# Decay attention with a gated convolution: loads in separate buffers, x's low part in two pieces, another order of the steps

## The chip, the core and the metric

The kernel runs on one core of a Trainium2 chip. A core has a tensor engine for matrix products (PE in the profile, its weight loads PEld), three engines for elementwise work (DVE, ACT and POOL), and a sync engine (SP), which here only issues the transfers between HBM and the core's SBUF. Matrix products land in PSUM, which has eight banks. The engines run side by side and wait for each other by semaphores. The metric is the device time in microseconds (us) of one execution.

## What is computed

Decayed linear attention over blocks of 64 positions, for 4 batches, 8 heads, 768 positions and head dimension 64; then, over the 512 channels that the heads make together, a causal convolution of 5 taps whose sigmoid gates `x @ w_val`, and a last product with `w_out`. `w_val`, `conv_w` and `w_out` come as float64, q, k, v and lam as float32.

```python
for b in range(nb):                                   # blocks of 64 positions
    intra = einsum('bhic,bhjc->bhij', qb, kb) * Dmask # lam^(i-j), lower triangle
    intra = einsum('bhij,bhjd->bhid', intra, vb)
    inter = einsum('bhid,bhde->bhie', qb * lam_pow, kv_state)
    out[:, :, sl] = intra + inter
    kv_state = lam_block * kv_state + einsum('bhsd,bhse->bhde', kb * rev_pow, vb)
...
x = out.transpose(0, 2, 1, 3).reshape(B, S, 512)
gate = sigmoid(sum(conv_w[k] * xp[:, k:k + S] for k in range(5)))
return (gate * (x @ w_val)) @ w_out
```

## The kernel before

The work is cut into 12 chunks (i = 0 to 11): chunk i holds 128 positions of one pair of batches, chunks 0 to 5 of the first pair and 6 to 11 of the second, where the state starts anew. Two chunks make a unit (un = 0 to 5), over which the convolution runs.

Every step is an entry of a plan with a name, an engine and the steps that it needs. The names, which the text below uses:

- `ld.i.0` and `ld.i.2` load 1 MB each: q and k transposed (kT), and v and k by positions. `wv.u` and `wo.u` load the halves of the weights, 1 MB each, and `cv` conv_w (20 KB).
- `s.i.u` are the scores on PE (`u` is a half of the heads; in chunks 0 to 2 each half is a step), `m.i...` their masking on DVE, `kd.i` the decay of k (on ACT in chunks 1, 2, 3, 4 and 6, otherwise on POOL), `st.i` the product of k and v on PE that updates the state, `up.i` the update on DVE, `fd.i` the fading of the state on POOL, `qd.i` the decayed q on POOL, `ia.i` and `in.i` the products within the block and with the state, on PE, into the bank `xp`.
- `x.i` copies x out of `xp` and `xh.i` makes its high part, both on ACT; `xl.i` is the rest, x minus the high part, on DVE in chunks 0 and 1 and on POOL in the others. The low part makes up for the precision that the fast product of the high part loses: `v.i.f` (256 columns) and `V.un.f` (512 columns) on PE multiply x by w_val as high times high, low times high and high times low, 12 matrix products for a step.
- `wv.u.k.e`, `n`, `s`, `w`, `v` on DVE, `r`, `m`, `h` on ACT and `l` on POOL turn a quarter of the float64 weights into a high part (`h`) and a low part (`l`).
- `t.un.f.kk` are the taps, the first on ACT and four on DVE, `sg` the sigmoid on ACT, `pb` the copy of a product out of PSUM on ACT, `ap` the gating on DVE, `hh` and `hl` the high and low part of the gated value, `p.i...` the product with w_out on PE, `ev` its copy on ACT and `o` its store.
- `f.n` is a filling product of zeros on PE. `WARM` products of zeros stand ahead of everything, and `f.0` and `f.1` between the first scores.

ORDER is a table of all these names, in which the steps are written out one after another. Each engine gets its own steps in that order and does them in that order: a step that waits holds up what is behind it on its engine, and a load on SP that waits for its buffer holds up all later loads and stores. After a colon stand the buffers that a step takes (`ld0`, `s0`, `u2`); it waits until the last reader of what was in them is done. SLOTS says how many there are of each. PSUM has four banks `u`, one `s` and one `xp` in use by name (`xp` and `s` take two banks each).

In the buffer `ld` lie all four parts of a chunk, so that neither of its loads can start before every reader of the chunk that was there is done, the last being the products `st` and `ia`.

## Time and profile before

| | |
|---|---|
| runs | 207.83, 209.11 and 210.05 us, median 209.11 |
| profiled execution | 208.13 us |
| its span, first to last instruction | 206.4 us (1.7 us lie around it) |
| busy: PE, PEld, DVE, ACT, POOL | 97%, 83%, 75%, 56%, 56% of the span |
| TensorE clock granted | 1.00 over the whole span |
| transfers | 36.15 MB; the DMA engines are full from about 5 to 40 us |

The page's first part gives the busy time of each engine. A matrix product's end is modelled, and products overlap; the starts of consecutive rows tell better what one of them takes. The answers are read by their times from the start of the span.

### The profile page before, as it was taken

What the parts mean: (1) busy time and instruction counts of PE and PEld (TensorE: products, weight loads), DVE (VectorE), ACT (ScalarE), POOL (GpSimd) and SP (SyncE); (2) the same over time, 40 slices, a digit from 0 to 9 for tenths busy, and PEclk for the clock granted to TensorE, in tenths of its full rate; (3) what the DMA queues carried; (4) which work ended last, traced back from release to release, by engine and by line L of the source; (5) the groups of instructions that cost most, each with busy time, mean ns of one, the idle gap of its engine ahead of it and who ended that gap; (6) DMA issues with size and microseconds to landing.
All of it is one profiled execution on the core that took longest, in us unless ns stands there. A gap on an engine that the chain in (4) does not pass through costs nothing.

```text
span 206.4 us, 7456 instructions
## 1 busy us (share of the span) xinstructions
PE 199.5 (97%) x3316; PEld 172.2 (83%) x3316; DVE 154.5 (75%) x240; ACT 115.2 (56%) x218; POOL 115.3 (56%) x103
## 2 busy tenths in 40 slices
PE   7879899999999999999999999999999999999995
PEld 7479699998999998989887978887987888888883
DVE  5797997999686999999989667817789289686000
ACT  2277779869664976676634925523565352642121
POOL 5276492788788499949975999662573400000000
DMA  5999999802878005994601159610020002210042
GB/s 174 418 426 422 422 427 426 351 10 67 346 268 345 8 3 157 347 404 124 251 4 54 56 173 391 256 51 3 3 77 27 0 3 102 103 51 0 3 176 79
DMA packets 7952, 36.15 MB, mean 175 GB/s; under 512 B 1136, under 2 KB 1392, under 8 KB 4336
## 3 DMA queue, kind: packets, MB, share of 16 engines
q1 hardware_dynamic: 7920, 35.68, 44.7%
q8 instruction: 26, 0.43, 0.8%
q14 instruction: 6, 0.05, 0.1%
HBM read 29.38 MB, written 6.29 MB: 173 GB/s over the span
## 4 chain that ended last, share of the span: by engine, by line
PE 87%; DMA 8%; SPq 2%; DVE 1%; POOL 1%; issue 0%; ACT 0%
PE op L837 33%; PE vp L728 33%; DMA w_raw<-in_w_val 8%; PE xp L510 5%; PE s L470 4%; PE xp L547 4%; PE st L572 4%; SPq L337 1%; PE xp L525 1%; POOL wv_lo L302 1%; PE so L460 1%; PE xp L536 1%; PE st L564 0%; PE fill L205 0%; DVE w_em L260 0%
## 5 line engine op out<-in xcount | busy, mean ns | idle before, releaser
L702 DVE SCALAR_TENSOR_TENSOR acc<-x,conv_sb,acc 128x512 f32<-128x512 f32 x96 | 70.7, 753 | 8.7 <-ACT acc L700 6.8
L728 PE MATMUL vp<-x_hi,wv_hi 128*128 128x256 f32 (+1 forms) x144 | 47.3, 328 | 0.0
L728 PE MATMUL vp<-x_hi,wv_lo 128*128 128x256 f32 (+1 forms) x144 | 45.9, 319 | 0.5 <-POOL wv_lo L302 0.5
L728 PE MATMUL vp<-x_lo,wv_hi 128*128 128x256 f32 (+1 forms) x144 | 45.8, 318 | 0.0
L844 ACT COPY o<-op 128x512 f32<-128x512 f32 (+1 forms) x25 | 14.3, 571 | 31.3 <-PE op L837 28.8
L676 POOL TENSOR_TENSOR x_lo<-x,x_hi 128x1024 fp32r<-128x1024 f32 x10 | 24.0, 2400 | 12.6 <-ACT x_hi L666 9.1
L837 PE MATMUL op<-wo_hi,hs 128*128 128x512 f32 x96 | 30.6, 400 | 0.0
L728 PEld LDWEIGHTS vp<-x_hi,wv_hi 128*128 128x128 f32 x144 | 27.3, 190 | 3.1 <-issue 0.2
L728 PEld LDWEIGHTS vp<-x_hi,wv_lo 128*128 128x128 f32 x144 | 27.3, 190 | 2.6 <-POOL wv_lo L302 0.7
L728 PEld LDWEIGHTS vp<-x_lo,wv_hi 128*128 128x128 f32 x144 | 27.4, 190 | 1.9
L420 POOL TENSOR_TENSOR qd<-ld,qdec_c 128x512 f32<-128x512 f32 (+1 forms) x18 | 23.4, 1308 | 4.8 <-DMA ld<-in_qkv 4.8
L707 ACT ACTIVATE g<-acc 128x512 f32<-128x512 f32 x24 | 14.4, 600 | 15.0 <-DVE acc L702 15.0
L584 POOL TENSOR_TENSOR sdec<-state,qdec_c 128x512 f32<-128x512 f32 x17 | 18.6, 1096 | 7.1 <-DVE state L581 7.1
L837 PEld LDWEIGHTS op<-wo_hi,hs 128*128 128x128 f32 x96 | 17.4, 188 | 3.9
L810 POOL TENSOR_TENSOR hs<-g,hs 128x512 fp32r<-128x512 f32 x12 | 15.4, 1296 | 9.0 <-ACT hs L799 9.0
L837 PE MATMUL op<-wo_hi,h_hi 128*128 128x512 f32 (+1 forms) x52 | 19.7, 379 | 0.0
L837 PE MATMUL op<-wo_hi,h_lo 128*128 128x512 f32 (+1 forms) x52 | 19.6, 377 | 0.0
L837 PE MATMUL op<-wo_lo,h_hi 128*128 128x512 f32 (+1 forms) x52 | 19.6, 376 | 0.0
L837 PE MATMUL op<-wo_lo,hs 128*128 128x512 f32 x48 | 18.8, 392 | 0.0
L700 ACT ACTIVATE acc<-x,conv_sb 128x512 f32<-128x512 f32 x24 | 16.7, 696 | 3.6 <-DVE state L581 3.2
L581 DVE TENSOR_TENSOR state<-st,sdec 128x512 f32<-128x512 f32 x17 | 11.7, 686 | 6.9 <-PE st L572 3.5
L799 ACT CAST h_hi<-vp 128x512 fp32r<-128x512 f32 x12 | 6.9, 590 | 16.2 <-DVE vp L774 16.2
(77 smaller groups left out, 354.9 us busy)
## 6 DMA issues: line engine op xcount, KB each, us to landing
ld<-in_qkv SPq DMA_DIRECT2D x24, 1024.0 KB, 8.9
out<-o SPq DMA_DIRECT2D x23, 256.0 KB, 2.1
w_raw<-in_w_val SPq DMA_DIRECT2D x2, 1024.0 KB, 11.4
w_raw<-in_w_out SPq DMA_DIRECT2D x2, 1024.0 KB, 14.3
out<-o SPq DMA_DIRECT2D x2, 128.0 KB, 1.7
conv_raw<-in_conv_w SPq DMA_DIRECT2D x1, 20.0 KB, 10.5
lam_bc<-in_lam SPq DMA_DIRECT2D x1, 4.0 KB, 1.7
```

The lines of the kernel that those rows point to most:

```text
L420: nc.gpsimd.tensor_tensor(out=s["qd"][:, hs, ms], in0=lds[i]["qT"][:, u].rearrange("p h (m i) -> p h m i", m=2)[:, :, ms], in1=qdec[:, hs, ...
L510: nc.tensor.matmul(s["xp"][rows(hh), b ^ m, b, g, :], lds[i]["v"][rows(m), b, h * D : (h + 1) * D], s["A"][rows(m), b, h, :], start=b == 0 ...
L581: nc.vector.tensor_tensor(out=state, in0=s["st"][m], in1=sdec, op=ALU.add)
L584: nc.gpsimd.tensor_tensor(out=sdec, in0=state, in1=qdec_c[:, :, n - 1 : n].to_broadcast([P, H, D]), op=ALU.mult)
L676: nc.gpsimd.tensor_tensor(out=s["x_lo"], in0=s["x"], in1=s["x_hi"].bitcast(F32), op=ALU.subtract)
L700: nc.scalar.mul(to, src, w)
L702: nc.vector.scalar_tensor_tensor(out=to, in0=src, scalar=w, in1=to, op0=ALU.mult, op1=ALU.add)
L707: nc.scalar.activation(xu[un]["g"][:, ct].rearrange("p u (b i) -> p b u i", b=NB2), xu[un]["acc", ct].rearrange("p b (u i) -> p b u i", u= ...
L728: nc.tensor.matmul(to, w[:, ct, fs], xx[:, ct], start=n_mm == 0, stop=n_mm == 3 * NT - 1)
L810: (nc.vector if direct else nc.gpsimd).tensor_tensor(out=to, in0=x["h", j, fs], in1=x["to", j, fs].bitcast(F32), op=ALU.subtract)
L837: nc.tensor.matmul(s["op", b, j][:, cols], hh, w[:, ft, cols], start=ft == 0 and n == 0, stop=ft == NT - 1 and n == 2,)
L844: nc.scalar.copy(s["o", b, j][:, cols], s["op", b, j][:, cols])
```

## The change

- The buffer `ld` (three, for all four parts of a chunk) becomes `lq` (q with kT) and `lv` (v with k), three of each; a load waits for the readers of its own half alone.
- `xl.i` on POOL, one subtraction of 1024 columns, becomes `xl.i.0` and `xl.i.1`, of 512 columns each. Every product with w_val still waits for both pieces of its chunk.
- The buffers of the output `o` are three and no longer two. `ident` is made in the buffer of `sdec`, which has no other use at that time.
- One filling product stays of three (FILL); in the new order it stands after both score steps of chunk 0.
- ORDER is another table of the same steps. Both loads of chunk 0 stand ahead of the first half of w_val, and `ld.2.0` ahead of `ld.1.2`.

The diff, cut: of the table one line of each stands here.

```diff
-FILL = 3
+FILL = 1
...
-SLOTS = {"ld": 3, "qd": 2, "A": 2, "x": 3, "xs": 2, "g": 2, "val": 4, "hs": 2, "o": 2, "s": 1, "xp": 1, "u": 4}
+SLOTS = {"lq": 3, "lv": 3, "qd": 2, "A": 2, "x": 3, "xs": 2, "g": 2, "val": 4, "hs": 2, "o": 3, "s": 1, "xp": 1, "u": 4}
...
-ld.0.0:ld0 wv.0:g0 ld.0.2 qe dm.0 ld.1.0:ld1 cv ld.1.2 dm.1 wv.1:g1 ld.2.0:ld2 f.0:u0 s.0.0:s0 f.1:u0 m.0.1.0:A0
+dm.0 ld.0.0:lq0 s.0.0:s0 s.0.1:u0,u1 qe dm.1 m.0.0.0:A0 ld.0.2:lv0 kd.0.0 wv.0:g0 ld.1.0:lq1 m.0.0.1:A1 m.0.1.0 f.0:u2
...
-    ident = const.tile([P, P], F32, name="ident")
+    sdec = const.tile([P, H, D], F32, name="sdec")
+    ident = sdec.rearrange("p h d -> p (h d)")[:, :P]
...
-        ld_buf[i] = Buf("ld")
-
-        cuts = (0, 2, 4)
-        for lo, hi in zip(cuts, cuts[1:]):
-
-            def go(i=i, lo=lo, hi=hi, src=qkv[pair, c]):
-                if i not in lds:
-                    t = buf("ld", "ld", [P, 4, 2, DM])
+        lds[i] = {}
+        for lo, tag in ((0, "lq"), (2, "lv")):
+            ld_buf[i, lo] = Buf(tag)
+
+            def go(i=i, lo=lo, tag=tag, src=qkv[pair, c]):
+                t = buf(tag, tag, [P, 2, 2, DM])
+                if lo:
+                    lds[i].update(v=t[:, :, 0], k=t[:, :, 1])
+                else:
...
-                nc.sync.dma_start(lds[i]["all"][:, lo:hi], src[:, lo:hi])
...
+                    lds[i].update(qT=hd[:, :, 0], kT=hd[:, :, 1])
+                nc.sync.dma_start(t, src[:, lo : lo + 2])
...
-        def split_x_lo(s=s, now=now, blocks=blocks):
+        def split_x_lo(u, s=s, now=now, blocks=blocks):
...
+                ts = slice(HU * u, HU * (u + 1))
                 nc.gpsimd.tensor_tensor(
-                    out=s["x_lo"], in0=s["x"], in1=s["x_hi"].bitcast(F32), op=ALU.subtract
+                    out=s["x_lo"][:, ts], in0=s["x"][:, ts], in1=s["x_hi"][:, ts].bitcast(F32), op=ALU.subtract
                 )
...
-        t_xs = add(f"xl.{i}", "DVE" if now else "POOL", split_x_lo, [t_xhi], x_bufs)
+        if now:
+            t_xs = [add(f"xl.{i}", "DVE", lambda f=split_x_lo: f(0), [t_xhi], x_bufs)]
+        else:
+            t_xs = [add(f"xl.{i}.{u}", "POOL", lambda u=u, f=split_x_lo: f(u), [t_xhi], x_bufs) for u in range(2)]
```

The order in which the program's instructions stand shows three places at the front. First the queue of SP, before (after the first load of `ld` and the first half of w_val, the pair of `ld` rows is v and k of chunk 0 and then q and kT of chunk 1):

```order
L173 DMA lam_bc<-in_lam 128x8
L337 DMA ld<-in_qkv 128x2048
L355 DMA w_raw<-in_w_val 128x2048
L337 DMA ld<-in_qkv 128x2048 x2
L370 DMA conv_raw<-in_conv_w 128x40
L337 DMA ld<-in_qkv 128x2048
L355 DMA w_raw<-in_w_val 128x2048
```

The same queue in the changed kernel (`lq` is q with kT, `lv` is v with k; the pair is chunks 1 and 2):

```order
L174 DMA lam_bc<-in_lam 128x8
L337 DMA lq<-in_qkv 128x2048
L337 DMA lv<-in_qkv 128x2048
L355 DMA w_raw<-in_w_val 128x2048
L337 DMA lq<-in_qkv 128x2048 x2
L337 DMA lv<-in_qkv 128x2048
L370 DMA conv_raw<-in_conv_w 128x40
L355 DMA w_raw<-in_w_val 128x2048
```

The first half of w_val moved from the second to the third megabyte, the second half from the sixth to the seventh, and the first load of chunk 1 stayed the fourth.

Second, PE's queue from its start, before (`s` and `so` are the scores of the two halves of the heads, `xp` at L525 the product within the block, `st` the update, `vp` the product with w_val):

```order
L186 MATMUL warm<-zero 128x128 x9
L205 MATMUL fill<-zero 128x512
L460 MATMUL s<-ld 128x128 x8
L205 MATMUL fill<-zero 128x512
L460 MATMUL so<-ld 128x128 x8
L525 MATMUL xp<-A,ld 64x128 x16
L564 MATMUL st<-ld 64x64 x16
L460 MATMUL s<-ld 128x128 x8
L460 MATMUL so<-ld 128x128 x8
L728 MATMUL vp<-x_hi,wv_hi 128x256
```

PE's queue in the changed kernel:

```order
L460 MATMUL s<-lq 128x128 x8
L460 MATMUL so<-lq 128x128 x8
L206 MATMUL fill<-zero 128x512
L525 MATMUL xp<-A,lv 64x128 x16
L460 MATMUL s<-lq 128x128 x8
L564 MATMUL st<-lv 64x64 x16
L460 MATMUL so<-lq 128x128 x8
L460 MATMUL s<-lq 128x128 x8
L460 MATMUL so<-lq 128x128 x8
L525 MATMUL xp<-A,lv 64x128 x16
L536 MATMUL xp<-qd,state 64x128 x16
L564 MATMUL st<-lv 64x64 x16
```

The first product with w_val (`vp`) now stands behind the scores of chunk 2 and all of the attention of chunk 1, and the first scores of chunk 1 stand ahead of the update of chunk 0.

Third, DVE's queue behind the masks of the decay, before (`A` is the masked scores, `w_em` and `w_v` belong to the conversion of w_val):

```order
L483 TENSOR_TENSOR A<-s,mask_c 128x512 x2
L260 TENSOR_SCALAR w_em<-w_raw 128x512
L267 TENSOR_SCALAR w_em<-w_raw 128x512
L483 TENSOR_TENSOR A<-so,mask_c 128x512
L280 SCALAR_TENSOR_TENSOR w_em<-w_raw,w_em 128x512
L267 TENSOR_SCALAR w_em<-w_raw 128x512
L483 TENSOR_TENSOR A<-so,mask_c 128x512
L286 SCALAR_TENSOR_TENSOR w_v<-w_raw,w_v 128x512
L292 TENSOR_TENSOR w_em<-w_v,w_em 128x512
```

DVE's queue in the changed kernel, from the row after the last of the four maskings of chunk 0:

```order
L261 TENSOR_SCALAR w_em<-w_raw 128x512
L268 TENSOR_SCALAR w_em<-w_raw 128x512 x2
L261 TENSOR_SCALAR w_em<-w_raw 128x512
L281 SCALAR_TENSOR_TENSOR w_em<-w_raw,w_em 128x512
L287 SCALAR_TENSOR_TENSOR w_v<-w_raw,w_v 128x512 x2
L293 TENSOR_TENSOR w_em<-w_v,w_em 128x512
L281 SCALAR_TENSOR_TENSOR w_em<-w_raw,w_em 128x512
L483 TENSOR_TENSOR A<-s,mask_c 128x512
L293 TENSOR_TENSOR w_em<-w_v,w_em 128x512
L483 TENSOR_TENSOR A<-s,mask_c 128x512
L579 COPY state<-st 128x512
L672 TENSOR_TENSOR x_lo<-xp,x_hi 128x4x128 x2
```

The four maskings of chunk 0 are now done before the first row of w_val, and the two quarters of the first half of w_val are converted one into the other ahead of the first masking of chunk 1.

Behind the front, PE's order has the attention products in fewer and longer stretches: counted over the whole queue, the products with w_val and w_out (L728 and L837) stand in 22 runs before and in 18 after, of which 2 and 1 lie in the front.

## Rows read from the trace of the kernel before

**Rows 1.** The page's first part: busy us (share) xinstructions.

```profile
PE 199.5 (97%) x3316; PEld 172.2 (83%) x3316; DVE 154.5 (75%) x240; ACT 115.2 (56%) x218; POOL 115.3 (56%) x103
```

**Rows 2.** What PE waited for: us in total, times, longest us.

```profile
PE xp L525 <- DMA ld<-in_qkv: 1.7, 1, 1.7
...
PE s L460 <- DMA ld<-in_qkv: 0.7, 2, 0.5
...
PE xp L510 <- issue: 0.4, 1, 0.4
```

**Rows 3.** PE, front: start us, us, what, xcount [idle before <-releaser].

```profile
6.22 1.16 PE L460 MATMUL s<-ld 64*128 64x128 f32 x16 [0.18 <-DMA ld<-in_qkv]
7.32 1.13 PE L205 MATMUL fill<-zero 128*128 128x512 f32 x2
...
11.34 1.97 PE L525 MATMUL xp<-A,ld 128*64 128x128 f32 x32 [1.67 <-DMA ld<-in_qkv]
...
20.99 1.10 PE L536 MATMUL xp<-qd,state 64*64 64x128 f32 x32
...
24.68 0.39 PE L728 MATMUL vp<-x_hi,wv_lo 128*128 128x256 f32 x1 [0.49 <-POOL wv_lo L302]
...
27.16 1.16 PE L470 MATMUL s<-ld 64*64 64x64 f32 x64
```

**Rows 4.** The transfer of the first half of w_val: start; then its us to landing.

```profile
1.64 0.42 SPq L355 DMA_DIRECT2D w_raw<-in_w_val  x1
...
w_raw<-in_w_val SPq DMA_DIRECT2D x1, 1024.0 KB, 7.1
```

**Rows 5.** DVE, front.

```profile
7.43 1.29 DVE L483 TENSOR_TENSOR A<-s,mask_c 128x512 f32<-128x512 f32 x2 [0.88 <-PE s L460]
8.78 0.43 DVE L260 TENSOR_SCALAR w_em<-w_raw 128x512 int32<-128x512 int32 x1
9.12 0.42 DVE L267 TENSOR_SCALAR w_em<-w_raw 128x512 int32<-128x512 int32 x1
...
20.13 0.76 DVE L260 TENSOR_SCALAR w_em<-w_raw 128x512 int32<-128x512 int32 x2 [1.30 <-DMA w_raw<-in_w_val]
```

**Rows 6.** ACT, front and after it.

```profile
11.93 1.23 ACT L236 COPY dmask<-mask_c 64x512 f32<-64x512 f32 x2
13.34 1.07 ACT L664 CAST x_hi<-xp 128x512 fp32r<-128x512 f32 x2 [0.17 <-PE xp L525]
...
16.73 2.46 ACT L401 ACTIVATE ld<-ld,mask_c 128x128 f32<-128x128 f32 x8
...
28.27 0.31 ACT L272 ACTIVATE w_em<-w_em,rebias 128x20 int32<-128x20 int32 x1 [1.45 <-DVE w_em L260]
...
41.63 0.62 ACT L298 CAST wo_hi<-w_em 128x512 fp32r<-128x512 f32 x1 [1.35 <-DVE w_em L292]
```

**Rows 7.** POOL, front.

```profile
13.77 1.28 POOL L413 TENSOR_TENSOR qd<-ld,qdec_c 128x512 f32<-128x512 f32 x1 [0.35 <-DMA ld<-in_qkv]
```

**Rows 8.** Chain that ended last, in order of time: start us, us, what.

```profile
54.01 1.63 PE vp L728 x12
55.64 0.62 PE xp L547 x32
56.27 0.47 PE xp L510 x32
56.73 7.39 PE vp L728 x60
```

**Rows 9.** POOL's groups: xcount, busy us, mean ns.

```profile
L676 POOL TENSOR_TENSOR x_lo<-x,x_hi 128x1024 fp32r<-128x1024 f32 x10 | 24.0, 2400 | 12.6 <-ACT x_hi L666 9.1 <-PE st L572 3.6
...
L810 POOL TENSOR_TENSOR hs<-g,hs 128x512 fp32r<-128x512 f32 x12 | 15.4, 1296 | 9.0 <-ACT hs L799 9.0
```

**Rows 10.** The end of the span: ACT's last row.

```profile
203.35 0.37 ACT L844 COPY o<-op 128x256 f32<-128x256 f32 x1 [0.85 <-PE op L837]
```

**Rows 11.** One microsecond in which PE stands still: busy us (instructions) by engine, clock.

```profile
10.00:11.00 1.00, 0.00 (x0) 0.00 (x0) 1.00 (x3) 0.45 (x1) 0.00 (x0) 1.00 1.03 434
```

More of the change, by code (lines that the diff above doesn't have):

```diff
@@ new lines @@
+hlw.4.0 p.7.1.0.0:u1 p.7.1.0.1 t.5.0.0:u2,g1 t.5.0.1 t.5.0.2 t.5.0.3 t.5.0.4 ev.7.1.0:o1 p.8.0.0.0:u3 t.5.1.0:u0
+o.7.1.0 t.5.1.1 t.5.1.2 t.5.1.3 p.8.0.0.1 o.6.0.0 ev.8.0.0:o2 sg.5.0 p.8.1.0.0:u1 p.8.1.0.1 ev.8.1.0:o1 p.9.1.0.0:u3
+p.9.1.0.1 t.5.1.4 sg.5.1 t.5.2.0:u2 t.5.3.0:u1 xl.10.1 o.8.1.0 ev.9.1.0:o0 o.9.1.0 t.5.3.1 t.5.2.1 t.5.3.2 t.5.3.3
+t.5.3.4 t.5.2.2 t.5.2.3 p.9.0.0.0:u0 t.5.2.4 p.9.0.0.1 sg.5.3 sg.5.2 ev.9.0.0:o1 xl.11.1 xl.10.0 V.5.0:u3 o.9.0.0
+apw.5.0 hhw.5.0:hs1 hlw.5.0:val3 V.5.1:u1 apw.5.1 hhw.5.1 V.5.2:u2 V.5.3:u0 o.8.0.0 hlw.5.1 apw.5.2 hhw.5.2
@@ L87 @@
+p.11.0.0.0:u3 hlw.5.2:val2 apw.5.3 p.10.0.0.0:u1 hhw.5.3 hlw.5.3 p.10.0.0.1 ev.10.0.0:o0 o.10.0.0 p.10.1.0.0:u2
+p.10.1.0.1 ev.10.1.0:o1 p.11.0.0.1 ev.11.0.0:o2 p.11.1.1.0:u0 p.11.1.1.1 o.10.1.0 o.11.0.0 p.11.1.0.0:u1 p.11.1.0.1
+ev.11.1.1:o0 o.11.1.1 ev.11.1.0:o1 o.11.1.0
 """
@@ L324, in plan_load @@
         pair, c = divmod(i, NC)
-        ld_buf[i] = Buf("ld")
-        cuts = (0, 2, 4)
-        for lo, hi in zip(cuts, cuts[1:]):
-            def go(i=i, lo=lo, hi=hi, src=qkv[pair, c]):
-                if i not in lds:
-                    t = buf("ld", "ld", [P, 4, 2, DM])
-                    hd = t.rearrange("p a w (h i) -> p a w h i", h=HP)
-                    lds[i] = {
-                        "all": t, "qT": hd[:, 0:2, 0], "kT": hd[:, 0:2, 1], "v": t[:, 2:4, 0], "k": t[:, 2:4, 1],
-                    }
-                nc.sync.dma_start(lds[i]["all"][:, lo:hi], src[:, lo:hi])
-            t = add(f"ld.{i}.{lo}", "DMA", go, [], [ld_buf[i]])
-            for part in range(lo, hi):
+        lds[i] = {}
[6 more added lines that the diff above has]
+                else:
+                    hd = t.rearrange("p a w (h i) -> p a w h i", h=HP)
+                    lds[i].update(qT=hd[:, :, 0], kT=hd[:, :, 1])
+                nc.sync.dma_start(t, src[:, lo : lo + 2])
+            t = add(f"ld.{i}.{lo}", "DMA", go, [], [ld_buf[i, lo]])
+            for part in range(lo, lo + 2):
                 t_ld[i, part] = t
@@ L435, in decay_attention_then_gated_conv @@
         t_qd = [
-            add(f"qd.{i}.{u}", "POOL", lambda u=u, f=scale_q: f(u), [t_ld[i, u], *t_qdec], [ld_buf[i], qd_buf])
+            add(f"qd.{i}.{u}", "POOL", lambda u=u, f=scale_q: f(u), [t_ld[i, u], *t_qdec], [ld_buf[i, 0], qd_buf])
             for u in range(0 if big and first else 2)
@@ L473, in scores @@
                             )
-            t_s = add(f"s.{i}.{us[0]}", "PE", scores, [t_ld[i, u] for u in us], [ld_buf[i], *s_bufs])
+            t_s = add(f"s.{i}.{us[0]}", "PE", scores, [t_ld[i, u] for u in us], [ld_buf[i, 0], *s_bufs])
             for b in range(NB2):
@@ L595, in decay_attention_then_gated_conv @@
                     f"ia.{i}.{u}", "PE", lambda u=u, f=intra_c: f(u), [t_in, *t_mask[u], t_ld[i, 2], t_ld[i, 3]],
-                    [xp_buf, A_bufs[u], ld_buf[i]],
+                    [xp_buf, A_bufs[u], ld_buf[i, 2]],
                 )
@@ L780, in decay_attention_then_gated_conv @@
                     f"V.{un}.{f}" if wide else f"v.{i}.{f}", "PE", lambda f=f, g=products: g(f),
-                    [t_v, *([gated[n - 1][8]] if wide else []), t_xs, *wv.done[f], *(t_gu if direct else ())], [vp_buf, xs_buf],
+                    [t_v, *(gated[n - 1][8] if wide else []), *t_xs, *wv.done[f], *(t_gu if direct else ())], [vp_buf, xs_buf],
                 )
```

108 lines of the change are left out of this document (50 added, 58 removed).

## The prediction

> **What bounds the kernel now.** I read the busy times first, then what PE waited for, then PE's timeline of the front, and last the chain that ended last. PE is busy 97% of the span and no other engine over 75% [rows 1]; the page warns that ends of products are modelled, so the waits decide. PE waited for loads three times, 2.4 us in all [rows 2], and the largest waits lie in the first 25 us: 1.67 us for v and k of chunk 0 at 11.34, and at 24.68 the 0.49 us for the low part of w_val [rows 3]. From there to its last product, which ACT copies out at 203.35 [rows 10], PE has one gap, 0.4 us that the profile puts to nothing ("issue") [rows 2]. So the change can win in three ways only: the front gets shorter, PE's own work gets shorter, or the stretch of 3.1 us behind the last product shrinks. It can lose wherever the new order makes PE wait in the 178 us that are now closed.
>
> **The front.** I set both orders against one mark: PE has done the scores of chunks 0 to 2, the attention of chunks 0 and 1, and two products with w_val. Before, that is the moment when the scores of chunk 4 begin, 27.16 [rows 3].
>
> The loads: q and kT of chunk 0 are there at 6.2, v and k of chunk 0 at 11.3, the load of chunk 1 at 13.7 [rows 3, 7]; the first half of w_val at 1.64 + 7.1 = 8.7 [rows 4]; the second half at 20.1 [rows 5]. A megabyte takes 2.5 us (8.7 to 11.3, 11.3 to 13.7). In the new queue v and k of chunk 0 come at 8.7 and the first half of w_val at 11.3; the first load of chunk 1 is the fourth megabyte as before, 13.7; then 16.2 for the scores of chunk 2, 18.7 for v and k of chunk 1, and 20.1 + 2.5 = 22.6 for the second half of w_val.
>
> PE by the new order: scores 6.2 to 8.5 (1.1 us each [rows 3]), the fill to 9.6. DVE masks from 7.43 [rows 5] and again from 8.5, one every 0.6 us, so it is done at 10.4; the products within the block then run from about 10.0 to 11.8, and not from 11.34 to 13.3. That is 1.5 us won, and it is given back at once: the next work, the scores of chunk 1, waits for 13.7. Then s.1.0 to 14.8, st.0 to 15.9, s.1.1 to 17.0.
>
> DVE has the conversion of two quarters of w_val ahead of the masks of chunk 1. From 11.3 to the end of m.1.1.0 stand four rows at 0.34 us (8.78 to 9.12 [rows 5]) and eight at 0.6: 11.3 + 1.4 + 4.8 = 17.5, and 0.1 for the last one's end, 17.6. The scores of chunk 2 need the bank that m.1.1.0 frees, so PE stands from 17.0 to 17.6. Then s.2 to 19.8. The bank xp is free when DVE has done up.0 and both halves of x_lo, 17.6 + 3 x 0.6 = 19.4, and the last masks of chunk 1 are done at 20.6. So ia.1 runs from 19.9 to 21.8, in.1 (1.0 us, 20.99 [rows 3]) to 22.9. On ACT, the first h follows DVE's fourth row of 0.6 us, at 15.2; h (0.6 us, like wo_hi), x.0 and x_hi (1.07 us each, taking the copy for as long as the cast), the second h and the cut of the masks (1.23 us) bring it to 19.7, and kd.1 (2.46 us) to 22.1 [rows 6], in time for st.1, 22.9 to 23.9. Two products with w_val, 24 rows, take 24 x 0.12 + 0.2 = 3.1 us by the runs below: 27.0. **The front gives 0.2 us.** Its bounds: with no wait on DVE the work behind 13.7 is 2.2 + 1.1 + 2.2 + 1.8 + 1.0 + 1.0 + 3.1 = 12.4 us, the mark is at 26.1 and the front gives 1.1 us; if w_val lands 1 us later than worked out, everything behind it shifts, 28.0, and it costs 0.8 us. I take 0.2, since DVE's chain is made of rows that the trace has.
>
> **Fewer runs.** An attention product behind a product of the other kind costs more than one behind its like: 0.62 us and 0.47 us for the same 32 rows [rows 8]. And a run of products with w_val has a start: 12 rows take 1.63 us and 60 take 7.39 [rows 8], so a row is 0.12 us and the rest, 1.63 - 12 x 0.12 = 0.19 us, is paid once. A break by attention costs 0.15 + 0.19 = 0.34 us at most, and 0.15 at least, if the 0.19 is paid at any change of the product. The count of runs behind the front falls from 20 to 17. Three times 0.3 us, **0.9 us less**, bounds 0.4 and 1.0; I take a value near the upper end, since these rows show both costs at the same break.
>
> **What costs nothing.** Two pieces of x_lo: a row of 512 columns with the same two kinds of operand takes 1.30 us on POOL, the whole takes 2.40 [rows 9], so ten chunks cost POOL 10 x 0.2 = 2 us of its 91 us of idle time; PE waits for no x_lo now [rows 2], and if that cover were gone it is 0.2 us a chunk, 2 us in all. The two fills: one stood between the scores of chunk 0, where PE then waited anyway [rows 3]; the other stands behind PE's last product, beside the copy out of PSUM at 203.35 [rows 10], and nobody waits for it. Separate buffers let loads start earlier, but PE's three waits for loads [rows 2] lie in the front, for data that no buffer holds up. The end is the same: two half-width products, two copies, two stores.
>
> **The sum.** 208.13 - 0.2 - 0.9 = 207.0 us for an execution like the profiled one. That one lies 1.0 us below the median of the runs; the middle of the four times that are known (207.83, 208.13, 209.11, 210.05) is 208.6, and I set the forecast there: 208.6 - 1.1 = **207.5 us**.
>
> **Rivals.** *The late weights come through* (slower). kd.1 now ends at 22.1 on ACT, 2.9 us later than 16.73 + 2.46 = 19.2 [rows 6], and ACT has the same work to do for the second half of w_val and for w_out, whose halves PE needs at nearly the same times. What absorbs it are ACT's waits behind the front, 1.45 and 1.35 us [rows 6], 2.8 us. If these remain, since ACT does its steps in order and waits for other engines, the 2.9 us reach PE through banks that ACT frees late (the copies `pb`, the sigmoids), between 30 and 60 us. From 1.1 us on the change is slower than before; in full it gives 207.5 + 2.9 = 210.4. Against it: by the front's working ACT is ready 0.8 us before st.1, and kd.2 and the next quarter of w_val come out 2 to 3 us before PE asks for them.
>
> *The front is closed.* If DVE's rows interlock better, the front gives 1.1, the runs 1.0, and the gap of 0.4 that nothing explains [rows 2] goes: 208.6 - 2.5 = 206.1. For it: the parts are bounds that I found above; against: all three together.
>
> *It does nothing.* The load ahead of w_val buys 1.5 us that PE loses again at 13.7, and if a break costs 0.15 and new small waits of 0.4 us stand in the order, the time stays at 208.6.
>
> *The clock.* PE stands still for 1.9 us at 11.8 in the new order, with two fills less. Before it stood 1.67 us [rows 3], a whole microsecond of it empty, and the granted clock stayed 1.00 [rows 11], so I leave it at full rate. Of the rows behind the gap 3.3 us of work (13.7 to 17.0) would be the first to suffer. [...]
>
> **How the numbers follow.** The forecast, 207.5 give or take 1.1, has 0.55; the closed front 0.18; nothing 0.10; the late weights 0.14; the clock 0.03. What a measurement of this kernel tells from no change is about 1%, 2.1 us. Below that line lie the closed front and some of the forecast's own spread: 0.29. Above it lie the clock and most of the late weights: 0.12. The rest, 0.59, is within 1%. The range leaves out the extreme of the late weights and of the closed front, with 0.5 us for the spread of the runs: 205.6 to 210.0.
>
> **What the profile would show.** Right: v and k waited for no longer at 11.3 but a wait of PE near 11.8 to 13.7 for the first load of chunk 1; a short one at 17.0 for DVE's mask; the first product with w_val at 23 to 24; the mark at 27; no wait of PE over 0.5 us behind it; the last product ending near 202. Wrong: waits of PE for ACT or for POOL's low part of w_val between 25 and 60 us; a granted clock below 1.00; a run of 12 products that takes 1.6 us whatever stands ahead of it.

## The result, and the profile after

Ten executions of each kernel on one chip: the kernel before takes 208.62 us (median; 207.67 to 211.03), the changed kernel 209.93 us (209.09 to 210.25). The ratio is 1.0058, 95% interval 1.0036 to 1.0081: 0.6% slower, where 0.5% faster was forecast. The profiled execution takes 209.98 us, 1.85 us more than that of the kernel before. (Ratios here and below leave out executions that the chip disturbed; the times in us are medians of all.)

What PE waited for in the changed kernel (us in total, times, longest), the answer to [rows 2]:

```profile
PE s L460 <- DMA lq<-in_qkv: 1.8, 2, 1.3
PE s L460 <- issue: 1.1, 1, 1.1
...
PE vp L732 <- issue: 1.0, 1, 1.0
PE xp L510 <- issue: 0.9, 1, 0.9
```

PE's timeline of the front (start, us, what, idle before and its releaser), the answer to [rows 3]:

```profile
6.53 2.08 PE L460 MATMUL s<-lq 64*128 64x128 f32 x16 [1.27 <-DMA lq<-in_qkv]
8.40 1.92 PE L460 MATMUL so<-lq 64*128 64x128 f32 x16
...
11.46 1.98 PE L525 MATMUL xp<-A,lv 128*64 128x128 f32 x32
13.99 1.16 PE L460 MATMUL s<-lq 64*128 64x128 f32 x16 [0.56 <-DMA lq<-in_qkv]
...
18.47 1.16 PE L460 MATMUL s<-lq 64*128 64x128 f32 x16 [1.14 <-issue]
...
27.60 1.16 PE L470 MATMUL s<-lq 64*64 64x64 f32 x64
```

And ACT's last row, the answer to [rows 10]:

```profile
205.21 0.37 ACT L848 COPY o<-op 128x256 f32<-128x256 f32 x1 [1.06 <-PE op L841]
```

These rows split the 1.85 us. The mark, where the scores of chunk 4 begin, is at 27.60 and no longer at 27.16: 0.44 us. From the mark to the last copy it takes 205.21 - 27.60 = 177.61 us, before 203.35 - 27.16 = 176.19: 1.42 us. Behind the copy nothing changed (208.2 - 205.21 = 3.0, before 3.05). The 1.42 us have an exact counterpart: PE's waits behind the mark that the profile puts to nothing ("issue") were one of 0.43 us and are two of 0.95 and 0.90, 1.85 in all. Taken off, the stretch is 175.76 us in either kernel.

The wait of 1.14 us at 18.47 is put to nothing as well, but it lies ahead of the mark and is of another kind. It stands at the start of a step, the scores of chunk 2, and ends 0.10 us after the mask on DVE that frees the bank of this step, at 17.70 + 0.67 = 18.37; the prediction had this wait, until 17.6:

```profile
17.70 0.67 DVE L483 TENSOR_TENSOR A<-s,mask_c 128x512 f32<-128x512 f32 x1
```

The two waits behind the mark, in PE's timeline:

```profile
45.65 0.28 PE L732 MATMUL vp<-x_hi,wv_lo 128*128 128x256 f32 x1
46.88 0.39 PE L732 MATMUL vp<-x_hi,wv_hi 128*128 128x256 f32 x1 [0.95 <-issue]
...
47.79 1.16 PE L470 MATMUL s<-lq 64*64 64x64 f32 x64
48.77 0.65 PE L547 MATMUL xp<-qd,state 64*64 64x64 f32 x32
49.24 0.57 PE L510 MATMUL xp<-A,lv 64*64 64x64 f32 x25
50.71 0.34 PE L510 MATMUL xp<-A,lv 64*64 64x64 f32 x7 [0.90 <-issue]
```

Both stand in the middle of a step, after 6 of the 12 products of v.2.2 and after 25 of the 32 of ia.3.1, where no semaphore is waited for. Between the two lie 6 + 64 + 32 + 25 = 127 products, each with a load of its weights: 254 instructions, and one other of PE's on record. The page's list of queues has one of instructions whose size fits PE's program (packets, MB, share of 16 engines):

```profile
q8 instruction: 26, 0.43, 0.9%
```

Each of the 26 packets has 16,384 bytes. PE's 3,312 products, as many weight loads and 41 other instructions on record, 6,665, are 256 to a packet. This fits a program that comes in blocks of 256 instructions, through the DMA engines that carry the loads, with the two waits one block apart. What these engines did there, windows of 5 us of the changed kernel (behind the five busy times: clock, DMA share, GB/s):

```profile
40.00:45.00 5.00, 5.00 (x155) 4.79 (x153) 3.78 (x6) 4.32 (x11) 2.07 (x2) 1.00 0.99 415
45.00:50.00 5.00, 3.85 (x137) 3.44 (x134) 3.92 (x6) 4.29 (x12) 2.93 (x3) 1.00 0.38 152
```

and of the kernel before:

```profile
40.00:45.00 5.00, 5.00 (x153) 4.80 (x152) 4.89 (x8) 3.01 (x6) 4.79 (x4) 1.00 0.12 48
45.00:50.00 5.00, 4.57 (x148) 4.27 (x147) 4.54 (x9) 4.07 (x12) 4.35 (x5) 1.00 0.03 7
```

From 40.5 to 50.5 us the DMA engines of the kernel before are nearly idle; in the changed kernel loads fill them from 39 to 47. In this stretch PE has the small products of chunks 3 and 5 and uses up a block in 2.6 to 2.8 us.

That gave the theory. **Instruction supply:** the transfer of a block starts about when PE begins the block ahead of it; where the DMA engines are full it waits behind the loads; where PE is through its block first, it stands still. **Clock**, for the 0.44 us of the front: the first two score steps, 2.08 and 1.92 us for 1.16, run at about half the rate. The rivals: the stalls belong to PE's order alone, or to another part of the change; the slow scores are paid back at the wait for chunk 1.

### The profile page after: what moved, and what is told of

It is laid out like the page before. It is cut to its first block, busy times and chain, and to the rows that moved or that the text cites. A ratio compares the mean times of both kernels' runs of the same rounds, so it can differ in the third digit from the quotient of the medians.

```text
span 208.2 us, 7454 instructions
## 1 busy us (share of the span) xinstructions
PE 199.3 (96%) x3312; PEld 173.1 (83%) x3312; DVE 152.2 (73%) x240; ACT 114.4 (55%) x218; POOL 114.8 (55%) x113
## 4 chain that ended last, share of the span: by engine, by line
PE 90%; DMA 5%; issue 2%; SPq 1%; ACT 0%; ACTq 0%
PE vp L732 34%; PE op L841 33%; DMA lq<-in_qkv 5%; PE xp L510 5%; PE xp L547 4%; PE s L470 4%; PE st L572 4%; PE xp L525 2%; PE st L564 2%; PE s L460 1%; PE xp L536 1%; PE so L460 1%; SPq L337 0%; SPq L355 0%; ACT o L848 0%
## 5 line engine op out<-in xcount | busy, mean ns | idle before, releaser
L732 PE MATMUL vp<-x_hi,wv_hi 128*128 128x256 f32 (+1 forms) x144 | 47.2, 328 | 1.0 <-issue 1.0
L677 POOL TENSOR_TENSOR x_lo<-x,x_hi 128x512 fp32r<-128x512 f32 x20 | 25.5, 1288 | 11.8 <-ACT x_hi L666 11.8
L584 POOL TENSOR_TENSOR sdec<-state,qdec_c 128x512 f32<-128x512 f32 x17 | 19.1, 1125 | 11.6 <-DVE state L581 11.5
L420 POOL TENSOR_TENSOR qd<-lq,qdec_c 128x512 f32<-128x512 f32 (+1 forms) x18 | 22.1, 1242 | 2.0 <-PE xp L547 1.2
L841 PEld LDWEIGHTS op<-wo_hi,hs 128*128 128x128 f32 x96 | 17.6, 188 | 3.9
L841 PE MATMUL op<-wo_hi,h_hi 128*128 128x512 f32 (+1 forms) x52 | 19.9, 382 | 0.0
## 6 DMA issues: line engine op xcount, KB each, us to landing
conv_raw<-in_conv_w SPq DMA_DIRECT2D x1, 20.0 KB, 15.3
```

The lines of the kernel that those rows point to most:

```text
L420: nc.gpsimd.tensor_tensor(out=s["qd"][:, hs, ms], in0=lds[i]["qT"][:, u].rearrange("p h (m i) -> p h m i", m=2)[:, :, ms], in1=qdec[:, hs, ...
L584: nc.gpsimd.tensor_tensor(out=sdec, in0=state, in1=qdec_c[:, :, n - 1 : n].to_broadcast([P, H, D]), op=ALU.mult)
L677: nc.gpsimd.tensor_tensor(out=s["x_lo"][:, ts], in0=s["x"][:, ts], in1=s["x_hi"][:, ts].bitcast(F32), op=ALU.subtract)
L732: nc.tensor.matmul(to, w[:, ct, fs], xx[:, ct], start=n_mm == 0, stop=n_mm == 3 * NT - 1)
L841: nc.tensor.matmul(s["op", b, j][:, cols], hh, w[:, ft, cols], start=ft == 0 and n == 0, stop=ft == NT - 1 and n == 2,)
```

## The experiments

Each was timed beside the kernel before on the same chip; the interval is that of the ratio to it.

**e1_fill**, the changed kernel with a fill ahead of its first scores:

```diff
-dm.0 ld.0.0:lq0 s.0.0:s0 s.0.1:u0,u1
+dm.0 ld.0.0:lq0 f.0:u0 s.0.0:s0 s.0.1:u0,u1
```

Expected: 

> The changed kernel with one filling product of zeros put back ahead of the first scores, where the kernel before had one. Theory of the clock: in the profile of the changed kernel PE stands still from 5.26 to 6.53 and its first two score steps then take 2.08 and 1.92 us, as at half the rate, where they took 1.16 each in the kernel before; with the fill they take about 1.2 each, the mark (scores of chunk 4 begin) moves from 27.60 to about 26.9, and the time falls by 0.6 to 0.8 us. Rival: the slow scores are paid back at the wait for the first load of chunk 1, the mark stays within 0.2 us, and so does the time. Theory of the instruction supply, besides: PE's two stalls that the profile puts to nothing (at 45.93 and 49.80) come two products earlier in PE's order, since two products more stand ahead of them, and keep a sum of about 1.9 us.

Measured 209.37 us, ratio 1.0029 (0.9988 to 1.0070). PE's timeline:

```profile
6.28 1.16 PE L460 MATMUL s<-lq 64*128 64x128 f32 x16
7.27 1.06 PE L460 MATMUL so<-lq 64*128 64x128 f32 x16
...
13.76 1.16 PE L460 MATMUL s<-lq 64*128 64x128 f32 x16 [2.31 <-DMA lq<-in_qkv]
14.86 1.95 PE L564 MATMUL st<-lv 128*64 128x64 f32 x32
16.74 1.91 PE L460 MATMUL so<-lq 64*128 64x128 f32 x16
...
27.41 1.16 PE L470 MATMUL s<-lq 64*64 64x64 f32 x64
...
46.53 0.39 PE L732 MATMUL vp<-x_lo,wv_hi 128*128 128x256 f32 x1 [1.03 <-issue]
...
50.08 0.35 PE L510 MATMUL xp<-A,lv 64*64 64x64 f32 x9 [0.43 <-issue]
```

and a microsecond of its windows (clock before the DMA share):

```profile
15.00:16.00 1.00, 1.00 (x22) 1.00 (x24) 1.00 (x3) 0.93 (x2) 0.27 (x2) 0.50 0.99 418
```

The first scores are fast, PE then stands 2.31 us for chunk 1, and now the clock falls: 0.50 and no longer 1.00, from 14.9 to 18.3, where the rows take 1.95 and 1.91 us, about what the scores took in the changed kernel (2.08 and 1.92). There the clock column says 1.00 beside rows of the same length, but the first record of the clock in that trace begins at 10.6 us, behind them; that their clock was low too is my estimate from the lengths. The mark moves by 0.19 us only; the rest of the 0.6 us that this kernel is below the changed one is a shorter second stall (0.43 us for 0.90), and the intervals of the two ratios overlap. So what the theory of the clock expected of the first scores came (1.16 and 1.06 us), and what it expected of the mark did not. The theory of the instructions had its sharpest test: two products more at the front, and the stalls come after 4 and 23 products where they came after 6 and 25.

**e2_before_nofill**, the kernel before without that fill:

```diff
-ld.2.0:ld2 f.0:u0 s.0.0:s0 f.1:u0 m.0.1.0:A0
+ld.2.0:ld2 s.0.0:s0 f.0:u0 m.0.1.0:A0
```

Expected: 

> The kernel before without the filling product ahead of its first scores. Theory of the clock: its first score steps, 1.16 us each, become about 2 us each; since PE there waits for v and k until 11.34, most of the 1.7 us is absorbed, and the kernel comes out 0 to 0.8 us slower, with the first masks of DVE 0.8 us later. Rival (the slow scores of the changed kernel come from its new buffers or from the loads beside them): the scores stay at 1.16 us.

Measured 209.17 us, ratio 1.0000 (0.9957 to 1.0042). Its profiled execution (210.19 us) shows the first scores at 2.08 us and the mark at 28.70, 1.5 us late. But the times of the twelve, one of 212.9 apart, fall in two groups, 207.6 to 208.6 and 209.8 to 210.7, as those of the kernel before do. So the slow scores need none of the changed kernel's loads or buffers, and one fill more or less there makes no difference that these times show. That the two groups are executions with slow and with fast first scores is not shown: only one was profiled.

**e5_warm** and **e6_before_warm**, more fills, so that PE doesn't stand still at the front: two behind the products of chunk 0 in the kernel of e1_fill, one in the 1.67 us gap of the kernel before.

```diff
-ld.4.0:lq0 ia.0.1 kd.0.1
+ld.4.0:lq0 ia.0.1 f.2:u0 f.3:u1 kd.0.1
```

```diff
-s.0.1:u0,u1 m.0.0.0
+s.0.1:u0,u1 f.2:u3 m.0.0.0
```

Expected of e5_warm: 

> The changed kernel with the fill ahead of the first scores and two more fills between the products within the block of chunk 0 and the scores of chunk 1, where PE stood 2.31 us with the first fill alone and then ran at half the rate from 14.9 to 18.5. Theory of the clock: the products from 13.8 to 18.5 take 1.1 us a step again, PE then waits for DVE's mask until about 17.7, and the mark moves from 27.41 to 26.5 or 26.8; the time falls by 0.6 to 0.9 us against the kernel with one fill. Rival (DVE's chain and not the clock sets the scores of chunk 2): the mark and the time stay. The stalls of PE's instructions come four products earlier still and keep their size.

Expected of e6_before_warm: 

> The kernel before with one more fill in the 1.67 us in which PE waited for v and k of chunk 0. Its times fall in two groups, 207.2 to 208.4 with a mean granted clock of 1.000, and 208.4 to 210.2 with 0.992, about as many of each. Theory of the clock (in the second group PE's clock falls once at the front, after that gap): all runs come in the first group, and the median falls from 208.5 to about 207.8. Rival (the two groups have another cause, such as the stall of PE's instructions): the groups stay as they are.

Measured of e6_before_warm: 208.12 us, ratio 1.0006 (0.9975 to 1.0037). The mean granted clock is 1.000 in all twelve executions, and ten of them lie between 207.7 and 208.5; of 30 executions of the kernel before in the first batch 13 had 0.991 or 0.992, with a median of 209.41 us against 207.82 for the 15 at 1.000. So one fall of the clock costs the kernel before about 1.6 us; over the batches of the experiments 37 of 109 executions have one, and with a fill in the gap none of twelve. That the fall lies behind this gap is argued, since no execution of the kernel before with a fall was profiled. The median gained less than expected, since in the batch of this run only 3 of 15 executions of the kernel before had a fall (208.22).

Measured of e5_warm: 210.87 us, ratio 1.0126 (1.0064 to 1.0187). Its mark and its waits:

```profile
17.53 1.16 PE L460 MATMUL s<-lq 64*128 64x128 f32 x16 [0.50 <-DVE A L483]
...
20.00 1.97 PE L525 MATMUL xp<-A,lv 128*64 128x128 f32 x32 [0.42 <-DMA lv<-in_qkv]
...
27.06 1.16 PE L470 MATMUL s<-lq 64*64 64x64 f32 x64
```

```profile
PE vp L732 <- issue: 1.9, 2, 1.7
...
PE op L841 <- issue: 1.0, 1, 1.0
```

At full clock the scores of chunk 2 begin at 17.53 behind DVE's mask and the mark is at 27.06: what the clock costs here is 27.41 - 27.06 = 0.35 us. It is all lost again. PE runs out of instructions 1.4 us sooner (44.25 against 45.65), the block comes only 0.7 us sooner (46.17 against 46.88), since loads hold it, and another stall appears at 76.

**e3_loads** and **e9_late**, the load of q and kT of chunk 5 moved ahead. e9_late was meant to hold back a second load, but SP issues a load as soon as its own queue and buffer allow, whatever stands between in the table: both programs issue the same (q and kT of chunk 6 at 37.83 and 37.85 us), so this is one kernel measured twice.

```diff
-v.1.3 kd.3.0 ld.5.2:lv2 xl.2.0 hi.1
+v.1.3 kd.3.0 ld.5.0:lq2 ld.5.2:lv2 xl.2.0 hi.1
...
-wo.0.0.r v.2.2:u0 ld.5.0:lq2 s.5.0:s0 kd.4.0
+wo.0.0.r v.2.2:u0 s.5.0:s0 kd.4.0
```

Expected of e3_loads: 

> The changed kernel with the load of q and kT of chunk 5 moved from behind the product v.2.2 to just ahead of the load of v and k of chunk 5, so that the three loads that fill the DMA engines from 38 to 45 us are issued earlier and apart. Theory of the instruction supply (PE's instructions come in blocks of 16 KB by the same DMA engines, and the block that PE lacked at 45.93 started only at 44.56, behind these loads): the stall of 0.95 us at 45.93 falls to 0.4 or less and the time by 0.5 to 0.9 us. Rival (the stall belongs to the order of the products, dense small ones, and not to the loads): it stays at 0.9 us and so does the time.

Expected of e9_late: 

> The changed kernel with two loads moved: q and kT of chunk 5 ahead as before, and q and kT of chunk 6 from ahead of the product v.2.3 to behind it, so that the DMA engines, full from 39 to 47 us in the changed kernel, are idle from about 42 to 50 us, as they are in the kernel before (40.5 to 50.5). Theory of the instruction supply (the block that PE needs next waits behind the loads): the first stall, 0.95 us, falls to 0.3 or less, the second stays at 0.5 to 1.2, and the time falls by 0.6 to 1.0 us against the changed kernel, to about 209.0. Rival (the stalls belong to PE's order alone): both stay and so does the time.

Measured 209.60 and 209.19 us, ratios 1.0032 (0.9993 to 1.0071) and 1.0040 (1.0004 to 1.0076). The first stall fell to 0.32 and 0.5 us, the second was 1.17 and 0.63. Loads did change the first stall. Against the changed kernel's 209.93 us the gain is 0.3 to 0.7 us, but the intervals of the ratios overlap. In one profile the first scores are slow (2.08 and 1.92 us), in the other the rows behind 15.3 are (scores of 2.08 us at 16.55), and the mark is 27.49 and 27.51: it makes no difference which of them are slow.

**e4_spread**, the scores of chunk 5 moved behind v.2.3:

```diff
-v.2.2:u0 ld.5.0:lq2 s.5.0:s0 kd.4.0
+v.2.2:u0 ld.5.0:lq2 kd.4.0
...
-wo.0.0.l v.2.3 ld.6.2:lv1
+wo.0.0.l v.2.3 s.5.0:s0 ld.6.2:lv1
```

Expected: 

> The changed kernel with the scores of chunk 5 moved behind the product v.2.3, so that fewer small attention products stand in a row between 46 and 50 us. Theory of the instruction supply (256 instructions of PE in a block, and a new block takes longer to come than 256 small products take to run): the second stall, 0.90 us at 49.80, goes or falls below 0.4, the first stays, and the time falls by 0.4 to 0.9 us, less 0.1 to 0.3 for one more break in the run of v. Rival (a stall of the product ia.3.1 by its own operands): it stays at that product.

Measured 212.06 us, ratio 1.0140 (1.0087 to 1.0193): slower. The second stall is gone from ia.3.1, and this one has come:

```profile
54.09 0.69 PE L572 MATMUL st<-lv 64*64 64x64 f32 x33
56.85 0.69 PE L572 MATMUL st<-lv 64*64 64x64 f32 x31 [2.08 <-issue]
```

From the first stall to this one lie 255 products, two blocks. Here the loads of chunks 6, 9 and 7 had the DMA engines (share 1.01 while the transfer was waited for), and PE, still for 2 us, got a lower clock behind it (0.50 from 57.8 to 61.2).

**e7_table** and **e10_joint**, the change in parts, in the old order: with the separate buffers, and without them (both have x_lo in pieces, three o and ident in sdec).

```diff
-ld.0.0:ld0 wv.0:g0 ld.0.2 qe dm.0
+ld.0.0:lq0 wv.0:g0 ld.0.2:lv0 qe dm.0
```

Expected of e7_table: 

> The changed program with the order of the kernel before: separate buffers for q with kT and v with k, x's low part in two pieces, three buffers of o and three fills, steps in the old order. Theory (the table alone makes the difference): the time is that of the kernel before within 0.3 us, with one short stall of PE's instructions near 48. Rival (the pieces or the buffers cost something, for instance by loads that start earlier and fill the DMA engines when PE's instructions are due): 0.5 to 1 us slower than before, with longer stalls.

Expected of e10_joint: 

> The kernel before with x's low part in two pieces, three buffers of o and ident in the buffer of sdec, but with the common buffers of q, kT, v and k, so the whole change but for the separate buffers and the table. Theory (of the change's parts the separate buffers alone cost something in the old order, 2 us and more in the run that had all of them): the time is that of the kernel before within 0.3 us and the DMA engines are idle from 40.5 to 50.5 us. Rival (the pieces of x's low part cost it): 2 us and more slower than before.

Measured: e10_joint 208.14 us, ratio 0.9985 (0.9948 to 1.0023); e7_table 213.05 us, ratio 1.0189 (1.0113 to 1.0265). PE's waits in e7_table:

```profile
PE vp L731 <- issue: 2.5, 1, 2.5
...
```

My theory that the table alone makes the difference fell. By the two ratios the separate buffers cost the old order 2.0%, some 4 us: loads that the common buffer held back until 50 us now fill the DMA engines from 41 to 47.3, the block that was due at 43.6 starts at 47.2, and PE stands 2.5 us. The profiled execution, 214.22 us, has two falls of the clock besides, from 13.3 and from 50.9 us; three others took 211.2 to 211.9 us. In the program with separate buffers the new table brings the ratio from 1.0189 to 1.0058, so it wins about two thirds of the cost back.

**e11_extra**, the kernel before with two useless transfers, 1 MB each:

```diff
+    scr = nc.dram_tensor("scr", (2, P, NT * DM), F32, kind="Internal").ap()
+    def spill():
+        for n, t in enumerate((wv.hi, wv.lo)[:2]):
+            nc.scalar.dma_start(scr[n], t.bitcast(F32).rearrange("p a b -> p (a b)"))
+    add("zz", "ACT", spill)
...
-wo.1.1.h t.0.0.0:u3,g0
+wo.1.1.h zz t.0.0.0:u3,g0
```

Expected: 

> The kernel before with two useless transfers of 1 MB each (the high and the low part of w_val to a spare place in HBM, which nothing reads), issued by ACT near 42 us ahead of its first tap, so that the DMA engines, idle there before, are full from about 44 to 49 us. PE's order and its instructions stay as they are. Theory of the instruction supply: the transfer of a block that began at 46.3 comes 1.5 to 3 us later, PE's stall at 48.16, 0.43 us, grows to 1.5 to 3 us at the same product, and the time rises by as much, to about 210. Rival (PE's stall has nothing to do with the DMA engines): the stall stays at 0.4 us and the time at 208.3.

Measured 209.46 us, ratio 1.0045 (1.0005 to 1.0085). The DMA engines are full from 42 to 47, and at the same product as before:

```profile
48.05 0.53 PE L510 MATMUL xp<-A,ld 64*64 64x64 f32 x24
49.84 0.34 PE L510 MATMUL xp<-A,ld 64*64 64x64 f32 x8 [1.26 <-issue]
```

1.26 us for 0.43, with PE's instructions untouched. That is somewhat less than expected: the transfers went at 42 and not 44, and the transfer of the block began 1.8 us after PE began the block ahead, where it was 1.2 us before. That transfers alone make the stall longer is shown by this run.

**e12_swap** and **e15_late9**, the loads of the changed kernel so ordered that the DMA engines are idle in the dense stretch: `ld.5.0` ahead, as in e3_loads, and `ld.6.0` back, as the first cut shows; e15_late9 moves one more load away.

```diff
-t.0.0.0:u3 ld.6.0:lq0 t.0.0.1 wo.0.0.h wo.0.0.l v.2.3 ld.6.2:lv1
+t.0.0.0:u3 t.0.0.1 wo.0.0.h wo.0.0.l v.2.3 ld.6.2:lv1 ld.6.0:lq0
```

```diff
-xl.3.1 ld.9.0:lq1 t.0.0.2
+xl.3.1 t.0.0.2
...
-ld.9.2:lv2 wo.1.0.l
+ld.9.2:lv2 ld.9.0:lq1 wo.1.0.l
```

Expected of e12_swap: 

> The changed kernel with the load of q and kT of chunk 5 moved ahead of v and k of chunk 5, as before, and q and kT of chunk 6 behind v and k of chunk 6, which waits for its buffer until about 50.5. So the DMA engines are idle from about 42 to 51 us. Theory of the instruction supply: the first stall, 0.95 us in the changed kernel, falls to 0.2 or less; the second stays between 0.4 and 1.2; the time is 209.0 or a little less. Rival (the stalls belong to PE's order alone): the first stays at 0.5 to 1.

Expected of e15_late9: 

> The kernel of e12_swap with the load of q and kT of chunk 9, which nobody needs before 90 us, moved behind the load of v and k of chunk 9. So the DMA engines are full from 50 to about 60.5 us and not to 63. Theory of the instruction supply: the block whose transfer began at 62.5 comes 2 us earlier, the stall of 1.7 us at 63 falls to 0.3 or less, none comes in its place before 75, and the time falls by 1.3 to 1.9 us, to about 208. Rival (each load that is moved only moves the stall): one of 1 us or more comes behind 75, where the load now lies, and the time stays at 209.4.

Measured of e12_swap: 209.41 us, ratio 1.0049 (1.0016 to 1.0083). Windows:

```profile
40.00:45.00 5.00, 5.00 (x153) 4.79 (x153) 3.63 (x7) 4.34 (x11) 1.82 (x2) 1.00 0.35 129
45.00:50.00 5.00, 5.00 (x151) 4.72 (x150) 4.97 (x8) 5.00 (x13) 4.36 (x4) 1.00 0.12 21
...
55.00:60.00 5.00, 5.00 (x98) 4.80 (x97) 4.88 (x8) 4.49 (x8) 4.48 (x5) 1.00 1.00 416
60.00:65.00 5.00, 3.25 (x125) 3.02 (x124) 0.76 (x2) 3.42 (x10) 4.13 (x4) 1.00 0.60 249
```

Both stalls are gone, the second too, which I had expected to stay; the loads that were held back now fill the engines from 50 to 63 us, and a stall of 1.7 us stands at 63, four blocks on. The time hardly moves.

Measured of e15_late9: 207.96 us (207.05 to 208.72), ratio 0.9950 (0.9918 to 0.9982), below both kernels. PE's waits, all of them, and ACT's last row:

```profile
PE s L460 <- DMA lq<-in_qkv: 3.7, 2, 2.3
PE warm L188 <- DVE zero L179: 1.1, 1, 1.1
```

```profile
203.22 0.37 ACT L848 COPY o<-op 128x256 f32<-128x256 f32 x1 [1.06 <-PE op L841]
```

No wait on "issue" is left. From the mark (27.42) to the last copy it takes 175.80 us, what the other two kernels take without their stalls (175.76).

**e13_swap_warm**, **e16_late9_warm**, **e14_apart** and **e8_best** put the fills of e5_warm, or other places of the scores of chunk 5, on top.

```diff
-v.2.2:u0 s.5.0:s0 kd.4.0
+v.2.2:u0 s.5.0:s0 v.2.3 kd.4.0
```

(this is e14_apart against e13_swap_warm; e8_best has the scores behind v.3.2 and the loads of chunks 7 and 9 later).

Expected of e13_swap_warm: 

> The kernel of e12_swap with the three fills of e5_warm at the front. There the fills moved the mark from 27.41 to 27.06, and the first stall grew to 1.7 us, as it would if the block that PE lacked came at a moment that the loads set and PE only reached it sooner. Theory: with the DMA engines idle the first stall stays at 0.3 or less, and the time is 0.4 to 0.6 us under that of e12_swap, 208.5; a second stall of 0.4 to 1.0 stays, and one near 76 of up to 1 us may come, where the loads of chunks 7 to 9 begin. Rival: the front's gain is eaten by longer stalls whatever the loads do, and the time is that of e12_swap or more.

Expected of e16_late9_warm: 

> The kernel of e15_late9 with the three fills of the front. Theory: 0.4 to 0.6 us less than that kernel, about 207.5, so below the kernel before, if no stall comes in place of the ones removed. Rival: as with e13_swap_warm a stall of 1 to 2 us comes near 77, in the first product with w_out, where the loads of chunks 7 to 9 begin while PE's next block is due; then 209 to 211.

Expected of e14_apart: 

> The kernel of e13_swap_warm with the product v.2.3, 12 matrix products of 256 columns, moved between the scores of chunk 5 and the products of chunk 3, so that PE takes about 3.8 us and not 2.7 for the 256 instructions between the two stalls. Theory: the second stall goes, for one more break of 0.1 to 0.3 us; no stall from 42 to 60 us, and 0.3 to 0.8 us less than e13_swap_warm, about 208. Rival: the stall comes at the next block instead, near 53 to 55 us, and the time stays.

Expected of e8_best: 

> The changed kernel with the three fills of the front, the load of q and kT of chunk 5 moved ahead as before, the scores of chunk 5 moved behind the product v.3.2, and two later loads (q and kT of chunks 9 and 7) moved back, so that they don't fill the DMA engines from 50 to 55 us. Theory of the instruction supply: the stall in the product within the block of chunk 3 goes, the first one stays below 0.4 us, and no new one over 0.5 us comes; with the front's 0.8 us the time is about 207.5 to 208. Rival (a stall comes wherever small products are dense, so moving them moves the stall): one of 1 us or more stands further behind, between 52 and 58 us, and the time is 209 to 210.

Measured: e13_swap_warm 211.53 us, ratio 1.0135 (1.0077 to 1.0193); e16_late9_warm 209.19, 1.0005 (0.9965 to 1.0044); e14_apart 212.19, 1.0182 (1.0132 to 1.0232); e8_best 219.92 (213.98 to 222.37). In e13 and e16 the rival came true: PE reaches 77 us sooner, and meets the loads of chunks 7 to 9 there, with 1.9 us in the first product with w_out in e13 and 1.8 in e16, whose executions spread from 207.7 to 212.3 us. In e14 no stall comes at 53 to 55, but four do from 59 to 78 (0.6, 1.4, 0.2 and 0.3 us). e8_best was far slower than its rival said, and has:

```profile
PE op L841 <- issue: 3.7, 1, 3.7
PE xp L547 <- issue: 3.2, 1, 3.2
PE vp L732 <- issue: 2.5, 2, 1.5
```

with a mean clock of 0.51 and 0.54 in the 5 us from 85 and from 60, behind the first two. The profile is of the longest of its six executions, so these sizes carry no argument here. Counted in PE's instructions, all stalls over 0.2 us of these four lie at the place of the changed kernel's first one or whole blocks behind it.

The packets of the instruction queue show the same in one table, which is worked out from the traces (us). A block begins 256 instructions ahead of the one that PE stopped at, or whole blocks from there. The share is that of the DMA engines between the first two times; the last column runs from the start of the last product ahead of the stop to the start of the next one, "-" where PE did not stop:

```
              PE begins   transfer of the   DMA    its    PE out of
              a block     next one starts   share  length instructions
before        45.13       46.30 (+1.2)      0.00   0.93   47.94 to 48.59
changed       43.04       44.56 (+1.5)      1.01   0.95   45.65 to 46.88
changed       46.88       48.03 (+1.2)      0.15   1.29   49.59 to 50.71
e11_extra     45.56       47.38 (+1.8)      0.94   1.08   48.36 to 49.84
e4_spread     51.07       54.44 (+3.4)      1.01   0.93   54.55 to 56.85
e7_table      43.58       47.21 (+3.6)      1.01   0.94   46.66 to 49.47
e12_swap      42.76       42.02 (-0.7)      -      1.22   -
e12_swap      58.90       62.54 (+3.6)      1.01   0.98   63.01 to 64.98
e15_late9     58.99       60.91 (+1.9)      1.01   0.98   -
```

PE goes on 1.3 to 1.5 us after the end of a transfer, in every row with a stall. A late transfer alone makes no stall: in the last row PE takes 4.3 us over the block ahead. In the kernel before, between 13 and 42 us, four transfers start 2.7 to 3.4 us late with full DMA engines (share 1.01), and PE takes 6.9 to 7.7 us over each of the blocks ahead.

## Why the prediction was wrong

**What bounds the kernel now.** The step that failed is here: the one gap that the profile put to nothing, 0.4 us at 48.16 [rows 2], was named and left without a cause, and so the sum had no term for it. The waits of that kind went from 0.43 to 1.85 us, and the runs show why: loads in the DMA engines when a block is due (e11_extra makes the wait longer in the kernel before, 1.26 us for 0.43; e15_late9 takes all of them from the changed kernel, with 2.0 us).

**What costs nothing.** Right on the pieces of x_lo: e10_joint has them and is not slower, and PE waits for no x_lo. Wrong on the separate buffers. "Separate buffers let loads start earlier, but PE's three waits for loads [rows 2] lie in the front" looked for what the earlier loads bring and not for what they meet: the guard of the old common buffer kept the DMA engines idle for ten microseconds in which PE needed them. Without the new table they cost some 4 us. On the fills it was right for the one at the end.

**The front**, forecast -0.2 us, came out at +0.44. Its term for the first scores failed, 1.1 us each: the fill that stays now stands behind them and no longer ahead, PE stood still until 6.53, and they took 2.08 and 1.92 us. With a fill ahead again (e1_fill) they take 1.16 and 1.06. Otherwise the working by steps was good: at full clock (e5_warm) the mark is at 27.06, worked out at 27.0, and the scores of chunk 2 begin at 17.53, worked out at 17.6. In part that was luck: the products within the block of chunk 1 begin at 20.00, worked out at 19.9, but what they waited for were v and k of chunk 1, which the working had at 18.7. The rival *The clock* was put too low, at 3 in 100 because the column of the granted clock stays at 1.00 in a gap of the kernel before [rows 11]. That one profile was of an execution without a fall. In e1_fill the clock fell behind a gap of 2.31 us, once, to 0.50 from 14.9 to 18.3, on the very rows that the rival named. No run shows the loss of more than 1% with which the clock is counted among the chances: there the fall costs the mark 0.35 us (27.41 for 27.06 in e5_warm). The clock is low for 3.4 us only, so the rows from 13.76 to the scores of chunk 2 take 4.7 us for 3.3 in e5_warm, and about 1 us of that falls on waits that PE has in any case, 0.50 for DVE's mask and 0.42 for v and k of chunk 1.

**Fewer runs**, forecast 0.9 us less, [rows 8] is a term that the traces don't show at all. Less their stalls the kernels take 175.76, 175.76 and 175.80 us from the mark to the last copy, with 20 runs of the products with weights or 17. I took the most that the rows allowed for each of two costs, and charged both to the same break. The prices themselves stand in the changed kernel's chain:

```profile
56.14 1.63 PE vp L732 x12
57.77 0.62 PE xp L547 x32
58.39 0.47 PE xp L510 x32
58.86 4.51 PE vp L732 x36
```

What failed is what they were multiplied by. The 0.19 was read on products of 256 columns, and of these 10 runs begin behind the mark in either kernel; the three that are gone are two with w_out and one of 512 columns with w_val. Behind the mark the attention products take 40.49 us for 40.71 before, and those with w_out 68.25 for 67.99: differences that one profile of each kernel can't settle.

**The rivals.** *The late weights* (0.14) did not come: behind the mark PE waits for neither ACT nor POOL. *The front is closed* and *It does nothing* lie below the result. None of the four was the mechanism that decided, so the chances were spread over the wrong cases. The level was right: the ten executions of the kernel before have a median of 208.62, I had set 208.6, and the range held the result at its upper end. The forecast of 207.5 is near what the change is worth once PE's instructions come in time, 207.96 (e15_late9), 0.5% less than before, but that is luck: of its two terms the front came out the other way (27.42 for 27.16) and the runs are not in the traces. What e15_late9 wins is the stall of 0.43 us, which it has not, and the kernel before's own falls of the clock, which cost e15_late9 little (medians of 208.0 us with one and 207.7 without).

**What stays open:** why the clock falls in some executions of the kernel before and not in others, and what makes a transfer start 1.2 us after the block ahead in one case and 0.7 us before it in another with idle DMA engines.
